# Attention and two feed-forward layers: adds out of PSUM in place of accumulating transfers, and part of a bit shift on ScalarE

## The chip, the cores and the metric

The kernel runs on one core of a Trainium2 chip. The metric is the device time of one execution in microseconds. The engines are TensorE (PE in the profile, with its weight loads as PEld), VectorE (DVE), ScalarE (ACT), GpSimd (POOL) and SyncE (SP). SP and POOL issue nearly all of the DMA transfers.

## The reference

```
# q, k, v: (4, 12, 448, 64) float32; w_in (768, 2048), w_out (2048, 768), all four weights float64
scores = 1/sqrt(64) * q @ k.T - log(448)
x = sigmoid(scores) @ v                      # heads side by side: (1792, 768)
h = x @ w_in;   x = (h - tanh(h)) @ w_out    # layer 0
h = x @ w_in2;  out = (s * relu(h)**2 + b) @ w_out2   # layer 1, float32 out
```

The weights come in as 64-bit numbers, and the kernel has to make float32 of them on the chip.

## The kernel before

**Two passes.** The four batches are taken two at a time. A pass first does the attention of two batches (12 pairs of heads, 24 heads), and then runs both feed-forward layers on their 896 tokens. Each layer goes through 16 slices of 128 hidden columns in four groups of four (`FG`). A group multiplies x by its four slices of w_in, applies the activation to get g, and multiplies g by its rows of w_out. What a group gives is added to an output y (layer 0, twelve pieces of 128x448) or z (layer 1, fourteen pieces of 128x384). In the first pass y and z lie in SBUF (both in the tile pool `yz`, so the trace calls both y in the first pass); in the second pass they are collected in device memory, in `acc`, for all but the last group.

**Products.** Every float32 product is made of three matmuls, for which each operand is split in two float32r parts: a rounded copy (`copy`, a CAST in the trace) and the difference (a subtraction on VectorE). The products with w_in, and in the second pass those with w_out too, are done by a scheme of seven products for eight blocks, which needs sums of blocks of the weights. VectorE forms these sums in place, in the buffer `wf` that holds a chunk as float32 (`w_sums`).

**Weights.** A chunk is 128 x 768 weights; a group needs eight, four of w_in and four of w_out. In the first pass `load` brings a chunk as 64-bit words into one of three `raw` buffers through SP. `conv` makes float32 of it: `y` is the view of the high words and `a` that of the low words. The high words are scaled by 2^-112 as if they were float32, which sets the exponent right; this goes to ScalarE or VectorE. The low words are shifted right by 29 bits, on VectorE. Two more VectorE instructions put the three pieces together in `wf`. Then `keep` stores the chunk in device memory, from where the second pass loads it (`f_key`). The in-place sums have to wait until that store has read `wf`. For layer 0's first chunks the sums are stored too (`wout_s`, `win_s`).

**Adding up.** `evict` in `out1` and `out2` takes a finished PSUM bank. In group 0 it is copied to y by ScalarE or VectorE. In the last group, and in the second pass, VectorE adds it to y in one instruction. In groups 1 and 2 of the first pass `add_on` is used: ScalarE or VectorE copies the bank to a buffer `t`, and GpSimd issues a transfer from SBUF to SBUF that adds t to y (24 transfers of 224 KB in layer 0 and 28 of 192 KB in layer 1).

**What sets the order.** The class `Plan` collects all operations with the keys they read and write and a cost in microseconds for each engine that can do them. For a transfer the cost is a pair: how long the queue is busy issuing it, and when it is done. `emit` then plays these costs through and writes down, engine by engine, the order in which the operations are issued; for an operation with two possible engines (`EITHER`) it picks one. TensorE's order is fixed; the costs decide what the others do when. All engines run their instructions strictly in that order. In the trace every instruction has line 85, that of the helper that records them, so rows are told apart by their tiles: `hs` is a PSUM bank of the layers, `two` and `one` those of the attention.

Of the kernel before, what the change touches and what calls it, by code (L numbers as in the profile page):

```python
# [9 lines left out]
F32 = mybir.dt.float32  # L10
F32R = mybir.dt.float32r
U32 = mybir.dt.uint32
AF = mybir.ActivationFunctionType
ALU = mybir.AluOpType
# [5 lines left out]
def tile_kernel(ctx, tc, q, k, v, w_in1, w_out1, w_in2, w_out2, s_in, b_in, out):  # L20
# [17 lines left out]
    B, H, S, D = q.shape  # L38
# [9 lines left out]
    FC = DF // P  # L48
    HM = DM // 2
# [5 lines left out]
    FG = 4  # L55
# [180 lines left out]
    def copy(e, o, t):  # L236
        (act.copy if e == "ACT" else dve.tensor_copy)(o, t)
# [287 lines left out]

    def half(nm, j, src, keys, sbuf=True):
        t, key, _ = xo[nm, j]
        do(EITHER, (0.46, 0.35 if sbuf else 0.54), lambda e: copy(e, t()[:, 0], src()), r=keys, w=[(*key, 0)])
        do("DVE", 0.54, lambda: dve.tensor_tensor(out=t()[:, 1], in0=src(), in1=t()[:, 0].bitcast(F32), op=ALU.subtract), r=[*keys, (*key, 0)], w=[(*key, 1)])

    def less(o, a, b, r, w):
# [41 lines left out]
    class Layers:  # L573
# [11 lines left out]
        def do(self, eng, cost, fn, r=(), w=()):  # L585
            do(eng, cost, fn, r, w)
# [14 lines left out]
        def conv(self, n):  # L601

            self.load(n)
            if n in self.f_of:
                return
            key = chunks[n]
            rk, k = self.raw_of.pop(n), self.f.take()
            self.f_of[n] = k
            r, t = raw_w[rk], f_t[k]
            y, a = r[:, :, 1], r[:, :, 0]  # L610

            def scale(e):
                if e == "ACT":
                    act.activation(y.bitcast(F32), y.bitcast(F32), AF.Copy, scale=2.0 ** -112)
                else:
                    dve.tensor_scalar(y.bitcast(F32), y.bitcast(F32), 2.0 ** -112, None, op0=ALU.mult)

            self.do(EITHER, (0.74, 0.47), scale, w=[("r", rk)])
            self.do("DVE", 0.47, lambda: dve.tensor_scalar(a, a, 29, None, op0=ALU.logical_shift_right), w=[("r", rk)])
            self.do("DVE", 0.88, lambda: dve.scalar_tensor_tensor(out=a, in0=y, scalar=3, in1=a, op0=ALU.logical_shift_left, op1=ALU.bitwise_or), w=[("r", rk)])  # L620
            self.do("DVE", 0.88, lambda: dve.scalar_tensor_tensor(out=t.bitcast(U32), in0=y, scalar=0x80000000, in1=a, op0=ALU.bitwise_and, op1=ALU.bitwise_or), r=[("r", rk)], w=[("f", k)])
            self.r.give(rk)

            self.keep(k, key)

        def keep(self, k, key):

            def fn():
                scratch[key] = dram.tile([P, WE], F32, name="w" + "_".join(map(str, key)))
                sp.dma_start(out=scratch[key], in_=f_t[k])  # L630

            self.do("SP", (1.9, 3.0), fn, r=[("f", k)], w=[("d", key)])

        def kept_sums(self, key):
            return key[1] == 0 and key[2] < (FG if key[0] == "in" else 2)
# [6 lines left out]
            return self.f_of.pop(n)  # L642

        def hi_lo(self, src, hi, lo, r, w, half=False):
            self.do(EITHER, (0.42, 0.3) if half else (0.74, 0.47), lambda e: copy(e, hi(), src), r=r, w=[w[0]])
            self.do("DVE", 0.47 if half else 0.88, lambda: dve.tensor_tensor(out=lo(), in0=src, in1=hi().bitcast(F32), op=ALU.subtract), r=[*r, w[0]], w=[w[1]])

        def w_whole(self, k):

# [475 lines left out]
            prod("3", "a", 1)  # L1125
            to("a", 0, 1, True)

        def add_on(self, bank, m, to, keys):

            k = self.t.take()  # L1130
            self.do(EITHER, (0.43, 0.54) if m == S else (0.38, 0.47), lambda e: copy(e, self.tt[k][:, :m], self.banks[bank][:, :m]), r=[("b", bank)], w=[("t", k)])
            self.do("POOL", (1.0, 7.0), lambda: pool.dma_start(out=to(), in_=self.tt[k][:, :m], accum_op=ALU.add), r=[("t", k)], w=keys)
            self.t.give(k)

        def out1(self, layer, grp, n, close):

            final = grp == FC // FG - 1
# [20 lines left out]
            def evict(hd, d):  # L1158
                dm = hd * 3 + d
                t = lambda i: ys_t["y"][dm][:, i]  # L1160
                yk = [cells(dm * T2 + i * S, S) for i in range(2)]
                for i in range(2):
                    bank = ps[hd, d, i]
                    if grp == 0:
                        self.do(EITHER, (0.43, 0.54), lambda e, bank=bank, i=i: copy(e, t(i), self.banks[bank]), r=[("b", bank)], w=yk[i])
                    elif not self.sb and 0 < grp < FC // FG - 1:
                        self.add_on(bank, S, lambda i=i: t(i), yk[i])
                    else:
                        self.do("DVE", 0.54, lambda bank=bank, i=i: dve.tensor_tensor(out=t(i), in0=self.banks[bank], in1=t(i), op=ALU.add), r=[("b", bank)], w=yk[i])
                    self.b.give(bank)  # L1170
                if d == 2:
                    for k in range(2):
                        self.w_done(*self.units.pop(n + 2 * hd + k))
                if not final:
                    return
                j = dm // 2
                p = self.tt
                if dm % 2 == 0:
                    k = self.y_t1 = self.t.take()
                    half("11", j, lambda: t(0), yk[0])  # L1180
                    less(lambda: p[k], lambda: t(1), lambda: t(0), [*yk[0], *yk[1]], [("t", k)])
                    half("t1", j, lambda: p[k], [("t", k)])
                    return
                k1, k2, k3, k4 = self.y_t1, *(self.t.take() for _ in range(3))
                b11, bk = (lambda: ys_t["y"][dm - 1][:, 0]), cells((dm - 1) * T2, S)
                half("21", j, lambda: t(0), yk[0])
                less(lambda: p[k2], lambda: t(1), lambda: p[k1], [*yk[1], ("t", k1)], [("t", k2)])
                half("t2", j, lambda: p[k2], [("t", k2)])
                less(lambda: p[k3], lambda: p[k2], b11, [("t", k2), *bk], [("t", k3)])
                half("t3", j, lambda: p[k3], [("t", k3)])  # L1190
                half("22", j, lambda: t(1), yk[1])
                less(lambda: p[k4], lambda: t(0), lambda: p[k2], [("t", k2), *yk[0]], [("t", k4)])
                half("t4", j, lambda: p[k4], [("t", k4)])
                for k in (k1, k2, k3, k4):
                    self.t.give(k)
# [16 lines left out]
        def out2(self, layer, grp, n, close):  # L1212
# [24 lines left out]
            def evict(hd, t):  # L1237
# [2 lines left out]
                ks = cells(t * DM + hd * HM, HM)  # L1240
                if grp == 0:
                    self.do(EITHER, (0.38, 0.47), lambda e: copy(e, zt(), self.banks[bank][:, :HM]), r=[("b", bank)], w=ks)
                elif not self.sb and 0 < grp < FC // FG - 1:
                    self.add_on(bank, HM, zt, ks)
                else:
                    self.do("DVE", 0.47, lambda: dve.tensor_tensor(out=zt(), in0=self.banks[bank][:, :HM], in1=zt(), op=ALU.add), r=[("b", bank)], w=ks)
                self.b.give(bank)
# [136 lines left out]
```

## Time and profile before

| | us |
|---|---|
| median of 3 runs | 1054.42 (1052.88 to 1054.45) |
| the profiled execution | 1049.27 |
| its span, first to last instruction | 1047.5 |
| TensorE busy | 1028.0 (98%) |
| VectorE busy | 892.0 (85%) |
| ScalarE busy | 601.1 (57%) |
| GpSimd busy | 187.9 (18%) |

The span is 1.8 us shorter than the execution. The attention of the first pass ends near 85 us, the layers of the first pass run from there to about 540 us, the attention of the second pass to about 620 us, and its layers to the end. A busy TensorE is not TensorE at its best, since matmuls are pipelined; where it waits shows in its idle time. Times in the windows view are sums over instructions of one engine within a stretch.

### The profile page before, as it was taken

The page shows a single profiled execution, that of the slowest core. Times are in us where ns is not written, and L with a number is a line of the kernel's source. Part 1 is how long each engine was busy: PE and PEld are TensorE (multiplying, and loading weights), DVE is VectorE, ACT ScalarE, POOL GpSimd, SP SyncE. Part 2 cuts the span into 40 slices and gives each one's busy share as a digit, 9 for nine tenths or more (in the row PEclk, how much of TensorE's full clock was granted, in tenths as well). Part 3 has the DMA queues.
Part 4 walks back from the last instruction along what each step waited for, and adds up shares of the span by engine and source line. Part 5 has one row for each costly group of instructions (what it writes and reads, how often), then busy time and mean ns, then how long its engine had stood idle before and what let it go on. Part 6 is the DMA issues. An engine that isn't in the chain of part 4 may idle for free.

```text
span 1047.5 us, 15848 instructions
## 1 busy us (share of the span) xinstructions
PE 1028.0 (98%) x5688; PEld 896.7 (86%) x5688; DVE 892.0 (85%) x1480; ACT 601.1 (57%) x990; POOL 187.9 (18%) x238
## 2 busy tenths in 40 slices
PE   8999999999999999899999899999999999999998
PEld 4557999898988999898985459999999999999998
DVE  4899989897999998898856689798887999898962
ACT  5776666464555665454426566656555466666650
POOL 4220001203000003122222100306060003061600
PEclk9999999999999999999999999999999999999999
DMA  6773567969722659879576503929497019293963
GB/s 154 201 189 121 166 198 208 281 193 276 213 71 98 187 178 231 235 196 284 137 227 152 179 16 123 233 92 213 104 224 215 31 38 225 80 211 84 214 170 106
DMA packets 137966, 176.92 MB, mean 169 GB/s; under 512 B 53760, under 2 KB 108800, under 8 KB 137888
## 3 DMA queue, kind: packets, MB, share of 16 engines
q1 hardware_dynamic: 111200, 135.82, 41.6%
q0 software_dynamic: 25888, 39.89, 22.0%
q8 instruction: 45, 0.74, 0.3%
q10 hardware_dynamic: 800, 0.20, 0.1%
q14 instruction: 33, 0.27, 0.1%
HBM read 103.02 MB, written 61.83 MB: 157 GB/s over the span
## 4 chain that ended last, share of the span: by engine, by line
PE 76%; DVE 14%; DMA 5%; issue 2%; ACT 1%; SPq 0%; DVEq 0%; ACTq 0%
PE hs L85 64%; PE two L85 6%; PE one L85 6%; DVE t L85 4%; DVE wf L85 3%; DVE w L85 2%; DVE raw L85 2%; DVE xo L85 1%; DVE g L85 1%; DMA win<-wf 1%; DMA raw<-in_moe_w_out_dram 1%; DVE y L85 1%; DMA raw<-in_moe_w_in_dram 1%; DMA wf<-wout 1%; ACT t L85 1%
## 5 line engine op out<-in xcount | busy, mean ns | idle before, releaser
L85 PE MATMUL hs<-xo,w 128*128 128x448 f32 x2016 | 423.7, 368 | 6.6 <-DVE t L85 5.7
L85 PEld LDWEIGHTS hs<-xo,w 128*128 128x128 f32 x2016 | 378.2, 188 | 45.5 <-DVE t L85 7.6
L85 PE MATMUL hs<-w,g 128*128 128x384 f32 x1290 | 228.1, 335 | 0.7 <-DVE w L85 0.6
L85 PE MATMUL hs<-g,w 128*128 128x448 f32 x1098 | 226.4, 366 | 0.0
L85 PEld LDWEIGHTS hs<-w,g 128*128 128x128 f32 x1290 | 224.1, 188 | 2.2 <-DVE w L85 0.9
L85 PEld LDWEIGHTS hs<-g,w 128*128 128x128 f32 x1098 | 206.1, 188 | 17.2 <-DVE g L85 0.3
L85 DVE TENSOR_TENSOR w<-wf,w 128x768 fp32r<-128x768 f32 (+1 forms) x216 | 187.7, 883 | 23.5 <-PE hs L85 11.9
L85 ACT COPY t<-hs 128x448 f32<-128x448 f32 (+2 forms) x239 | 120.1, 515 | 111.1 <-PE hs L85 99.8
L85 ACT CAST w<-wf 128x768 fp32r<-128x768 f32 (+1 forms) x177 | 137.2, 781 | 77.5 <-DVE wf L85 58.5
L85 POOL DMA_DIRECT2D acc<-t x106 | 93.6, 1227 | 318.0 <-ACT t L85 157.1
L85 POOL DMA_DIRECT2D y<-t x52 | 46.1, 985 | 371.0 <-ACT t L85 177.4
L85 DVE TENSOR_TENSOR g<-t,g 128x448 fp32r<-128x448 f32 (+2 forms) x170 | 98.6, 596 | 6.7 <-ACT g L85 6.1
L85 DVE TENSOR_TENSOR wf<-wf 128x384 f32<-128x384 f32 x168 | 93.3, 556 | 12.6 <-DMA win<-wf 7.4
L85 ACT CAST g<-t 128x448 fp32r<-128x448 f32 (+2 forms) x147 | 79.9, 552 | 33.4 <-DVE t L85 31.7
L85 ACT ACTIVATE af<-two,nlogs 128x896 f32<-128x896 f32 (+1 forms) x96 | 85.2, 919 | 8.5 <-PE two L85 6.2
L85 DVE TENSOR_TENSOR t<-hs,t 128x448 f32<-128x448 f32 x114 | 70.2, 619 | 6.2 <-PE hs L85 4.1
L85 ACT ACTIVATE raw<-raw 128x768 f32<-128x768 f32 x60 | 55.6, 926 | 33.3 <-DMA raw<-in_moe_w_out_dram 23.4
L85 DVE SCALAR_TENSOR_TENSOR raw<-raw 128x768 uint32<-128x768 uint32 x64 | 61.2, 957 | 5.5 <-ACT raw L85 3.7
L85 ACT ACTIVATE t<-t,b_sb,s_sb 128x448 f32<-128x448 f32 x64 | 48.0, 761 | 25.4 <-DVE t L85 25.1
L85 DVE TENSOR_TENSOR t<-t 128x448 f32<-128x448 f32 (+1 forms) x98 | 58.8, 603 | 4.1 <-ACT t L85 3.8
L85 DVE SCALAR_TENSOR_TENSOR wf<-raw 128x768 uint32<-128x768 uint32 x64 | 60.7, 953 | 0.7
L85 PE MATMUL two<-qt,kt 64*128 64x448 f32 x396 | 51.4, 384 | 0.1
(79 smaller groups left out, 710.8 us busy)
## 6 DMA issues: line engine op xcount, KB each, us to landing
raw<-in_moe_w_in_dram SPq DMA_DIRECT2D x32, 768.0 KB, 5.7
raw<-in_moe_w_out_dram SPq DMA_DIRECT2D x32, 768.0 KB, 7.9
wf<-wout SPq DMA_DIRECT2D x36, 384.0 KB, 6.6
win<-wf SPq DMA_DIRECT2D x32, 384.0 KB, 3.5
wout<-wf SPq DMA_DIRECT2D x32, 384.0 KB, 6.3
wf<-win SPq DMA_DIRECT2D x32, 384.0 KB, 4.3
acc<-t POOLq DMA_DIRECT2D x51, 224.0 KB, 7.7
acc<-t POOLq DMA_DIRECT2D x55, 192.0 KB, 8.0
```

Source lines behind the costliest of these rows:

```text
L85: return lambda *a, **kw: tc.keep_in_program_order(getattr(self.engine, name)(*a, **kw))
```

## The change

Three things change. In groups 1 and 2 of the first pass a finished bank is added to y by VectorE, as in the last group, and `add_on` is gone. The shift of the low words may be done by ScalarE too: it reads the word as a number, multiplies by 2^-29 x (1 - 2^-16), takes away 0.5 - 2^-14 and rounds to a whole number on writing, which leaves the top three bits. And seven costs that the planner uses are other numbers.

```diff
     def half(nm, j, src, keys, sbuf=True):
-        do(EITHER, (0.46, 0.35 if sbuf else 0.54), ...)
+        do(EITHER, (0.46, 0.38 if sbuf else 0.6), ...)
...
         def conv(self, n):
...
-            self.do(EITHER, (0.74, 0.47), scale, w=[("r", rk)])
-            self.do("DVE", 0.47, lambda: dve.tensor_scalar(a, a, 29, None, op0=ALU.logical_shift_right), w=[("r", rk)])
+            self.do(EITHER, (0.83, 0.47), scale, w=[("r", rk)])
+
+            def top(e):
+                if e == "ACT":
+                    act.activation(a, a, AF.Copy, bias=-0.5 + 2.0 ** -14, scale=2.0 ** -29 * (1 - 2.0 ** -16))
+                else:
+                    dve.tensor_scalar(a, a, 29, None, op0=ALU.logical_shift_right)
+
+            self.do(EITHER, (0.83, 0.47), top, w=[("r", rk)])
...
         def keep(self, k, key):
...
-            self.do("SP", (1.9, 3.0), fn, r=[("f", k)], w=[("d", key)])
+            self.do("SP", (1.9, 5.2), fn, r=[("f", k)], w=[("d", key)])
...
         def hi_lo(self, src, hi, lo, r, w, half=False):
-            self.do(EITHER, (0.42, 0.3) if half else (0.74, 0.47), ...)
-            self.do("DVE", 0.47 if half else 0.88, ...)
+            self.do(EITHER, (0.42, 0.5) if half else (0.74, 0.47), ...)
+            self.do("DVE", 0.52 if half else 0.88, ...)
...
-        def add_on(self, bank, m, to, keys):
-
-            k = self.t.take()
-            self.do(EITHER, (0.43, 0.54) if m == S else (0.38, 0.47), lambda e: copy(e, self.tt[k][:, :m], self.banks[bank][:, :m]), r=[("b", bank)], w=[("t", k)])
-            self.do("POOL", (1.0, 7.0), lambda: pool.dma_start(out=to(), in_=self.tt[k][:, :m], accum_op=ALU.add), r=[("t", k)], w=keys)
-            self.t.give(k)
-
...
             def evict(hd, d):
...
-                    elif not self.sb and 0 < grp < FC // FG - 1:
-                        self.add_on(bank, S, lambda i=i: t(i), yk[i])
                     else:
                         self.do("DVE", 0.54, lambda bank=bank, i=i: dve.tensor_tensor(out=t(i), in0=self.banks[bank], in1=t(i), op=ALU.add), r=[("b", bank)], w=yk[i])
...
             def evict(hd, t):
...
-                elif not self.sb and 0 < grp < FC // FG - 1:
-                    self.add_on(bank, HM, zt, ks)
                 else:
                     self.do("DVE", 0.47, lambda: dve.tensor_tensor(out=zt(), in0=self.banks[bank][:, :HM], in1=zt(), op=ALU.add), r=[("b", bank)], w=ks)
```

With new costs and other operations the planner writes another order on VectorE, ScalarE, SP and POOL; TensorE's stays. Three places matter below. The first is on VectorE, late in group 1 of layer 1 of the first pass (422 to 431 us of the trace). The names are buffers: raw is a chunk of 64-bit words, wf a chunk as float32, w its split parts, hs a PSUM bank, y the output; the rows with 128x3x128 are the in-place sums. Before:

```order
L85 SCALAR_TENSOR_TENSOR wf_83<-raw_106 128x768
L85 COPY t_100<-hs_949 128x384
L85 SCALAR_TENSOR_TENSOR wf_84<-raw_104 128x768
L85 TENSOR_TENSOR w_78<-wf_83,w_992 128x768
L85 TENSOR_TENSOR w_79<-wf_84,w_79 128x384
L85 TENSOR_SCALAR raw_105<-raw_105 128x768 x2
L85 SCALAR_TENSOR_TENSOR raw_105<-raw_105 128x768
L85 TENSOR_TENSOR wf_84<-wf_84 128x3x128
L85 TENSOR_TENSOR wf_84<-wf_83,wf_84 128x3x128
L85 SCALAR_TENSOR_TENSOR wf_81<-raw_105 128x768
L85 TENSOR_TENSOR wf_83<-wf_84,wf_83 128x3x128
L85 TENSOR_TENSOR wf_83<-wf_83 128x3x128
```

Here one bank is copied by VectorE, the TENSOR_SCALAR row is two shifts, and the four sums in wf_84 and wf_83 stand among conversions. The same place in the changed kernel:

```order
L85 TENSOR_TENSOR y_140<-hs_962,y_140 128x384
L85 SCALAR_TENSOR_TENSOR raw_104<-raw_104 128x768
L85 SCALAR_TENSOR_TENSOR wf_84<-raw_104 128x768
L85 SCALAR_TENSOR_TENSOR wf_83<-raw_106 128x768
L85 TENSOR_TENSOR y_140<-hs_956,y_140 128x384
L85 TENSOR_TENSOR y_140<-hs_957,y_140 128x384
L85 TENSOR_TENSOR w_78<-wf_83,w_1001 128x768
L85 TENSOR_TENSOR w_79<-wf_84,w_79 128x384
L85 TENSOR_TENSOR y_140<-hs_960,y_140 128x384
L85 SCALAR_TENSOR_TENSOR raw_105<-raw_105 128x768
L85 SCALAR_TENSOR_TENSOR wf_81<-raw_105 128x768
L85 TENSOR_TENSOR wf_84<-wf_84 128x3x128
```

The shifts are gone from here, and four adds of a bank into y stand between the conversions, ahead of the weight parts and sums that follow them.

The second place is on SP, at the boundary of the passes. rawqkv is a set of q, k and v for the second pass's attention, wout_..._s are stored sums of w_out, and wf<-win_0_1 is a load of weights for layer 0 of the second pass. Before, behind the last q and k loads:

```order
L85 DMA rawqkv_4619<-in_k_dram 64x2x64
L85 DMA out_0_dram<-y_140 128x384
L85 DMA wout_0_0_1_s_4953<-wf_82 128x768
L85 DMA wout_0_1_0_s_4968<-wf_83 128x768
L85 DMA wout_0_1_1_s_4981<-wf_84 128x768
L85 DMA wf_82<-win_0_1_0_583 128x768
L85 DMA wf_83<-win_0_0_0_s_831 128x768
L85 DMA wf_84<-win_0_1_0_s_856 128x768
```

The three stores of sums stand behind the loads of q and k and right ahead of the weight loads that need their buffers. In the changed kernel the stores stand far ahead, among the last output stores of the first pass, in front of all those loads of q and k:

```order
L85 DMA wf_81<-win_0_0_0_697 128x768
L85 DMA wout_0_0_1_s_4434<-wf_82 128x768
L85 DMA out_0_dram<-y_140 128x384
L85 DMA wout_0_1_0_s_4456<-wf_83 128x768
L85 DMA out_0_dram<-y_140 128x384 x3
L85 DMA wout_0_1_1_s_4486<-wf_84 128x768
L85 DMA rawqkv_4208<-in_q_dram 128x3x64 x2
L85 DMA rawqkv_4208<-in_q_dram 64x2x64
L85 DMA rawqkv_4208<-in_k_dram 128x3x64 x2
L85 DMA rawqkv_4208<-in_k_dram 64x2x64
```

At the place where they were there are now only the weight loads:

```order
L85 DMA out_0_dram<-y_140 128x384
L85 DMA wf_82<-win_0_1_0_560 128x768
L85 DMA wf_83<-win_0_0_0_s_857 128x768
L85 DMA wf_84<-win_0_1_0_s_923 128x768
L85 DMA out_0_dram<-y_140 128x384
```

The load wf_82<-win_0_1 now follows an output store, and the stores whose buffers it and the next two loads use are all earlier.

The third place is on VectorE, where that load is used (579 to 588 us of the trace). two is a PSUM tile with q and k of the next pair of heads, which go to qt and kt in two parts each; one is the PSUM tile of a pair's result, whose bank is free once xo and y are written from it. Before:

```order
L85 CAST qt_4611<-two_4623 128x448
L85 CAST kt_4613<-two_4623 128x448
L85 COPY t_103<-two_4623 128x512
L85 TENSOR_TENSOR qt_4611<-two_4623,qt_4611 128x448
L85 TENSOR_TENSOR kt_4613<-two_4623,kt_4613 128x448
L85 CAST w_78<-wf_82 128x384
L85 TENSOR_TENSOR w_78<-wf_82,w_78 128x384
L85 TENSOR_TENSOR one_4626<-one_4626,t_102 128x224
L85 CAST xo_87<-one_4626 128x448
L85 TENSOR_TENSOR xo_87<-one_4626,xo_87 128x448
```

The half-width cast of wf_82 stands behind qt and kt of the next pair, with two instructions between it and xo. In the changed kernel:

```order
L85 CAST w_78<-wf_82 128x384
L85 CAST qt_4560<-two_4572 128x448
L85 CAST kt_4562<-two_4572 128x448
L85 COPY t_103<-two_4572 128x512
L85 TENSOR_TENSOR qt_4560<-two_4572,qt_4560 128x448
L85 TENSOR_TENSOR kt_4562<-two_4572,kt_4562 128x448
L85 TENSOR_TENSOR w_78<-wf_82,w_78 128x384
L85 TENSOR_TENSOR w_80<-wf_83,w_79 128x768
L85 TENSOR_TENSOR one_4575<-one_4575,t_102 128x224
L85 CAST xo_87<-one_4575 128x448
L85 TENSOR_TENSOR xo_87<-one_4575,xo_87 128x448
```

It now stands ahead of qt and kt, and a full-width difference of wf_83 has come between it and the work on one.

## Rows read from the trace of the kernel before

**Rows 1.** Part 1 of the page: busy us (share of the span) xinstructions.

```profile
PE 1028.0 (98%) x5688; PEld 896.7 (86%) x5688; DVE 892.0 (85%) x1480; ACT 601.1 (57%) x990; POOL 187.9 (18%) x238
```

**Rows 2.** TensorE's timeline: start, length, instructions [idle before <-what ended it].

```profile
205.89 15.14 PE L85 MATMUL hs<-xo,w 128*128 128x448 f32 x72 [0.62 <-ACT t L85]
...
314.24 19.71 PE L85 MATMUL hs<-xo,w 128*128 128x448 f32 x93 [0.98 <-DVE t L85]
...
334.69 1.51 PE L85 MATMUL hs<-w,g 128*128 128x384 f32 x5 [0.57 <-DVE w L85]
...
433.57 16.42 PE L85 MATMUL hs<-xo,w 128*128 128x448 f32 x72 [2.83 <-DVE t L85]
...
487.37 3.88 PE L85 MATMUL hs<-xo,w 128*128 128x448 f32 x18 [0.80 <-DVE t L85]
...
505.03 2.09 PE L85 MATMUL hs<-xo,w 128*128 128x448 f32 x9 [0.37 <-DVE t L85]
...
589.13 4.46 PE L85 MATMUL one<-af,rawqkv 128*64 128x448 f32 x20 [2.94 <-DVE y L85]
```

**Rows 3.** Windows: us, engines' busy us (xinstructions), PEclk, DMA share, GB/s.

```profile
434.00:436.00 2.00, 2.00 (x10) 1.83 (x9) 2.00 (x4) 1.58 (x2) 0.00 (x0) 0.77 1.02 404
436.00:438.00 2.00, 2.00 (x7) 1.80 (x6) 1.86 (x4) 0.53 (x1) 0.00 (x0) 0.50 1.06 408
```

**Rows 4.** The same view, longer stretches of the first pass.

```profile
180.00:215.00 35.00, 34.38 (x169) 31.40 (x168) 29.94 (x47) 18.99 (x30) 9.56 (x11) 1.00 1.03 271
400.00:438.00 38.00, 35.17 (x186) 33.76 (x185) 30.21 (x44) 16.80 (x28) 12.48 (x14) 0.96 1.07 285
465.00:495.00 30.00, 28.83 (x157) 27.33 (x156) 25.54 (x40) 12.72 (x19) 10.38 (x12) 1.00 1.09 285
270.00:340.00 70.00, 68.29 (x331) 61.43 (x331) 69.62 (x119) 39.35 (x66) 0.00 (x0) 1.00 0.35 110
```

**Rows 5.** DMA, 180 to 215 us (packets, MB, share; median us to landing), then 275:345.

```profile
q0 software_dynamic: 1728, 2.75, 45.2%
...
raw<-in_moe_w_out_dram SPq DMA_DIRECT2D x4, 768.0 KB, 11.4
...
win<-wf SPq DMA_DIRECT2D x4, 384.0 KB, 6.4
...
raw<-in_moe_w_out_dram SPq DMA_DIRECT2D x4, 768.0 KB, 5.3
...
win<-wf SPq DMA_DIRECT2D x4, 384.0 KB, 3.6
```

**Rows 6.** Chain of waits ahead of two stalls: start, us, what.

```profile
424.38 4.96 DMA win<-wf
...
483.27 12.13 DMA raw<-in_moe_w_out_dram
```

**Rows 7.** Groups by shape: xcount | busy us, mean ns | idle before.

```profile
L85 DVE TENSOR_TENSOR y<-hs,y 128x448 f32<-128x448 f32 x26 | 15.5, 619 | 0.5 <-PE hs L85 0.4
...
L85 DVE TENSOR_TENSOR y<-hs,y 128x384 f32<-128x384 f32 x14 | 7.7, 555 | 10.1 <-PE hs L85 10.1
...
L85 DVE TENSOR_SCALAR raw<-raw 128x768 uint32<-128x768 uint32 x64 | 35.7, 558 | 6.8 <-DMA raw<-in_moe_w_out_dram 4.3 <-DMA raw<-in_moe_w_in_dram 2.5
...
L85 ACT ACTIVATE raw<-raw 128x768 f32<-128x768 f32 x60 | 55.6, 926 | 33.3 <-DMA raw<-in_moe_w_out_dram 23.4 <-DMA raw<-in_moe_w_in_dram 9.5
...
L85 ACT CAST w<-wf 128x768 fp32r<-128x768 f32 x147 | 122.4, 836 | 66.7 <-DVE wf L85 53.7 <-PE hs L85 10.4 <-DMA acc<-t 1.1
...
L85 ACT ACTIVATE t<-t,b_sb,s_sb 128x448 f32<-128x448 f32 x64 | 48.0, 761 | 25.4 <-DVE t L85 25.1
```

**Rows 8.** The pass boundary: VectorE's and SyncE's timeline.

```profile
585.77 0.55 DVE L85 CAST w<-wf 128x384 fp32r<-128x384 f32 x1 [3.93 <-DMA wf<-win]
...
577.22 1.70 SPq L85 DMA_DIRECT2D wout_s<-wf  x3
581.44 0.32 SPq L85 DMA_DIRECT2D wf<-win  x1
```

More of the change, by code (lines that the diff above doesn't have):

```diff
@@ L527, in half @@
         t, key, _ = xo[nm, j]
-        do(EITHER, (0.46, 0.35 if sbuf else 0.54), lambda e: copy(e, t()[:, 0], src()), r=keys, w=[(*key, 0)])
+        do(EITHER, (0.46, 0.38 if sbuf else 0.6), lambda e: copy(e, t()[:, 0], src()), r=keys, w=[(*key, 0)])
         do("DVE", 0.54, lambda: dve.tensor_tensor(out=t()[:, 1], in0=src(), in1=t()[:, 0].bitcast(F32), op=ALU.subtract), r=[*keys, (*key, 0)], w=[(*key, 1)])
@@ L644, in hi_lo @@
         def hi_lo(self, src, hi, lo, r, w, half=False):
-            self.do(EITHER, (0.42, 0.3) if half else (0.74, 0.47), lambda e: copy(e, hi(), src), r=r, w=[w[0]])
-            self.do("DVE", 0.47 if half else 0.88, lambda: dve.tensor_tensor(out=lo(), in0=src, in1=hi().bitcast(F32), op=ALU.subtract), r=[*r, w[0]], w=[w[1]])
+            self.do(EITHER, (0.42, 0.5) if half else (0.74, 0.47), lambda e: copy(e, hi(), src), r=r, w=[w[0]])
+            self.do("DVE", 0.52 if half else 0.88, lambda: dve.tensor_tensor(out=lo(), in0=src, in1=hi().bitcast(F32), op=ALU.subtract), r=[*r, w[0]], w=[w[1]])
         def w_whole(self, k):
```

## The prediction

> **What bounds the kernel now.** I read part 1 of the page first. TensorE is busy 1028.0 of 1047.5 us, so only the 19.5 us in which it stands still, and what a lowered clock adds, can be won; VectorE at 85% and ScalarE at 57% have room on average [rows 1]. So the next view was TensorE's timeline, for the matmuls that had to wait [rows 2]. The reader should see that the stalls are few, that they lie in the first pass (85 to 540 us) and at its end, and that nearly all were ended by a VectorE or ScalarE result. In the first pass they are 0.62 us at 205.9, 0.98 at 314.2, 0.57 at 334.7, 2.83 at 433.6, and three from 0.80 to 0.37 us between 487 and 505 (0.80, 0.37, 0.37). At the pass boundary 2.94 us end at 589.1. After the 2.83 us stall the granted clock was 0.77 for 2 us and 0.50 (the 1.2 GHz level) for the next 2 us, though matmuls ran all the time [rows 3]: 2 x 0.23 + 2 x 0.50 = 1.46 us more.
>
> What comes before these stalls? The stretches that end in the first, the 2.83 and the 0.80 us stall (and a fourth like them between 235 and 270) have the DMA engines full (1.03 to 1.09 of 16 engines) and VectorE not full: 30.21 of 38 us in the one that ends worst [rows 4]. In them run the accumulating transfers. In 180 to 215 the software queue, that is those transfers, takes 45.2% of the DMA engines' time, and a load of 64-bit w_out words lands after 11.4 us, a store of a converted chunk after 6.4 us. In 275 to 345, where no accumulating transfer runs, the same load takes 5.3 us and the same store 3.6 us [rows 5]. The chain of waits runs through such transfers right ahead of two of the stalls: 4.96 us of a win store before 433.6, 12.13 us of a w_out load before the last ones [rows 6]. So these stalls are late weights: VectorE can't form the sums in a wf buffer before its store has read it, nor start a chunk before its load lands. The stretch 270 to 340 is the other kind: DMA at 0.35, VectorE at 69.62 of 70 us, and 0.98 + 0.57 us lost.
>
> **The change part by part.**
> *The 52 accumulating transfers go.* Each was a copy out of PSUM by ScalarE or VectorE and a transfer; now VectorE adds the bank to y itself: 28 x 555 ns + 24 x 619 ns = 30.4 us more [rows 7]. In the instruction order 39 copies leave ScalarE and 13 leave VectorE (9 of 384 columns, 4 of 448), which at the same durations is 7.5 us less for VectorE. GpSimd's issuing goes too; nobody on the path waits for it.
> *The shift of the low words.* All 64 were VectorE's, at 558 ns; in the new order 17 instructions of that form are left on VectorE instead of 68 (4 of the 68 were scalings), and ScalarE has 111 on raw instead of 60. So VectorE loses 51 x 0.558 = 28.5 us, and its sum for the kernel is 30.4 - 7.5 - 28.5 = -5.6 us. ScalarE gains 51 times a form that the trace doesn't show (whole numbers in and out). Its nearest row is the scaling of the same words at 926 ns; a cast of the same size at 836 ns is the lower bound, and the activation with scale and bias at 761 ns for 448 columns, or 1.30 us for 768, the upper. I take 0.926: 47.2 us (42.6 to 66.6). Even with none of the 39 copies taken off, ScalarE then stands at 648 us, 62%, and at the upper bound at 668 us, 64%: it does not become the bound. The two ScalarE passes of a chunk now follow each other where VectorE's shift ran beside the scaling, so a chunk is ready up to 0.93 us later. I cost that at nothing: it is hidden by the three raw buffers that load ahead, and in the four stretches by a load that lands 6.1 us sooner. Without that cover it would be 0.93 us at each of the four other groups' ends, 3.7 us.
> *VectorE group by group.* The two groups of each layer that had the transfers get 12 x 0.619 = 7.4 us (layer 0) or 14 x 0.555 = 7.8 us (layer 1), less 3.6 us of shifts (51 / 8 x 0.558) and 1.2 or 2.5 us of copies. The stretches go from 29.94 to about 32.6 of 35 us, from 30.21 to 31.9 of 38 and from 25.54 to 27.3 of 30 [rows 4]. They still fit. The final group of layer 0 gets only the relief of 3.6 us.
> *The planner's costs* (a store of a chunk 5.2 instead of 3.0, a scaling 0.83 instead of 0.74, a half-width cast 0.50 instead of 0.30) are nearer to the durations [rows 5, 7]. They move the sums in wf behind more other work, among it the new adds, as the rows of the order in the section on the change show.
>
> *The sum.* Term A, the stalls behind slow transfers: 0.62 + 2.83 + 0.80 + 0.37 + 0.37 = 4.99 us and 1.46 us of clock, 6.45 us. I take all of it, since what makes these transfers slow loses nearly half of its DMA time; what is late next there is VectorE.
> *Term B*, the full stretch of layer 0: 1.55 us against a relief of 3.6 us; I take half, 0.8, because an order written anew does not put its relief where the stall was.
> *Term C*, what is new: a bank is now freed by VectorE alone, in its order, ahead of weight work behind it. The trace shows that form twice without transfers: layer 0's final group lost 1.55 us at a full VectorE, and the same timeline has no stall in layer 1's final group, from 505.0 on. So 0 to 1.55 us for each of four groups, 0 to 6.2; with VectorE at 84 to 93% I take 0.25 each, 1.0.
> *Term D*, the pass boundary: the three sum stores that held up the load of the next weights (issued at 577.22) stand in the new order ahead of the second pass's loads of q and k, and no longer behind them, so the load, issued at 581.44 [rows 8], can go right behind the last output store, about 4.2 us sooner. But the half-width cast that waits for it (3.93 us idle on VectorE) now stands ahead of the next pair's five instructions on PSUM and not behind them, and a full-width difference has come in, all of it before the result that TensorE waited for. Gain and loss about cancel: 0, with -2.94 - 1.46 = -4.4 us and, if TensorE waits for those casts too, some +1 as its ends.
>
> -6.45 - 0.8 + 1.0 + 0 = -6.25 us. On the profiled execution's 1049.27 us (span 1047.5 and 1.8 around it) that is 1043.0. The median of the runs, 1054.42, lies 5.15 above that execution, and I move the difference over: **1048.2 us**. With C at its least and B whole it is 1046.4 (-8.0), with C at its most and B at nothing 1054.2.
>
> **The rivals.**
> *The transfers were not the limit.* In the four stretches the DMA engines moved 271 to 285 GB/s, but in 436 to 438 us the core moved 408 GB/s [rows 3, 4]. If bytes are the measure, there was room, the late weights come from the order of loads and stores, and A stays: -0.8 + 1.0, so 1054.6 us, no change. Against it stand the same load at 11.4 and 5.3 us. For it: landings depend on when a load is issued, and the order is new. The Trainium skill, "Perfetto Trace Analysis", section "Identifying the Most-Contended Engine", speaks for this rival: it wants the DMA side judged by memory bandwidth used, and not by occupancy, as sixteen engines make occupancy mislead. By that rule 66 to 70% of the rate reached elsewhere is no bound and the forecast would be 1054.6; the trace agrees that the rate was below its best, and not that the transfers were quick.
> *VectorE becomes the bound where the adds are* (the slower side). Its place is the four group ends, where PSUM adds, each waiting for TensorE, stand in VectorE's order among the chunk conversions. If one of them waits, the weights behind it come late, as at 433.6. Price: 2.83 us at each of the four ends, 11.3 us, in place of A: -6.45 - 0.8 + 11.3 = +4.1, so 1058.5 us (1064.3 with 1.46 us of clock at each). It decides from the point where VectorE's work fills the stretch, as it did in 270 to 340; I work out 84 to 93%, so it takes 7% more work or waiting than that. For it: 465 to 495 comes out at 27.3 of 30.
> *The boundary stall goes as well.* The stores are out of the way and the load lands early enough: 1046.4 - 4.4 = 1042.0 us.
> *The shift does not move, or ScalarE is late with the casts behind it*: the order shows that 51 move; ScalarE at 62% leaves no price beyond the 3.7 us above.
>
> **How the numbers follow.** A measurement of this kernel tells 0.2%, 2.1 us, from no change. The forecast has 0.57 (1045.5 to 1051.5), the boundary case 0.12 (down to 1042.0), transfers not the limit 0.19 (1052.3 to 1056.5), VectorE as bound 0.12 (above that). All of the first two is faster than 1052.3, and I count a little of the third below it: faster 0.70, same 0.18, slower 0.12. For 8 in 10 I take 1042.5 to 1055.5.
>
> **What would show it.** Right: in the stretches around 180 to 215 and 400 to 438 the DMA share well below 1, w_out loads landing near 5.5 us, no matmul waiting 2.83 us near 433 and the clock at 1.00 there; VectorE near 92% busy in them; ScalarE's rows on raw 111 near 926 ns; the stall near 314 smaller or gone. Wrong: TensorE stalls of over 1 us that end on a VectorE add into y or on a w behind one (the slower rival), or loads that land sooner with the stalls still there (the first rival). A boundary stall gone would show D mis-sized.

## The result and the profile after

The changed kernel takes 1033.81 us (median of 4 runs, 1033.22 to 1035.47) against 1053.65 us of the kernel before beside it (4 runs, 1051.61 to 1054.45): a ratio of 0.9823, 95% interval 0.980 to 0.9845. It is faster by 19.8 us. The prediction had the direction and its main mechanism, but its 1048.2 us held only about a third of the gain, and its range reached down only to 1042.5.

The profiled execution took 1033.57 us (span 1031.8, mean granted clock 1.0). Part 1 of its page, to set against [rows 1]: TensorE stands still for 8.2 us of the span in place of 19.5.

```profile
PE 1023.6 (99%) x5688; PEld 896.3 (87%) x5688; DVE 884.8 (86%) x1469; ACT 617.1 (60%) x1001; POOL 141.8 (14%) x186
```

The windows (us, then busy us of PE, PEld, DVE, ACT and POOL with their counts, granted clock, DMA share, GB/s), which answer to [rows 3, 4]:

```profile
180.00:215.00 35.00, 35.00 (x175) 32.43 (x174) 32.35 (x49) 19.74 (x29) 0.00 (x0) 1.00 0.64 201
...
400.00:438.00 38.00, 38.00 (x202) 36.20 (x202) 36.03 (x58) 22.36 (x32) 0.00 (x0) 1.00 0.57 182
...
465.00:495.00 30.00, 30.00 (x155) 28.03 (x154) 27.14 (x42) 19.03 (x29) 3.03 (x5) 1.00 0.50 156
...
270.00:340.00 70.00, 69.85 (x348) 64.18 (x347) 69.29 (x118) 41.94 (x67) 0.00 (x0) 1.00 0.29 90
...
434.00:436.00 2.00, 2.00 (x12) 1.81 (x11) 2.00 (x4) 2.00 (x4) 0.00 (x0) 1.00 0.25 46
```

TensorE fills every one of the stretches to within 0.15 us, at the full clock; the DMA share is 0.50 to 0.64 where it was 1.03 to 1.09; VectorE is at 32.35 of 35 us (the prediction said 32.6) and 27.14 of 30 (27.3). In 400 to 438 it is at 36.03 where 31.9 was forecast, because TensorE got through 202 matmuls there in place of 186, and VectorE's work came with them. The stretch of the kernel before that holds the same 202 matmuls has 34.57 us of VectorE, so the change added 1.5 us where 1.7 was forecast:

```profile
404.94:447.39 42.45, 39.62 (x202) 37.49 (x202) 34.57 (x54) 21.62 (x36) 10.12 (x12) 0.96 0.90 234
```

The DMA view of 180 to 215 us shows loads and stores as quick as those of a stretch without accumulating transfers [rows 5]:

```profile
raw<-in_moe_w_out_dram SPq DMA_DIRECT2D x3, 768.0 KB, 5.1
...
win<-wf SPq DMA_DIRECT2D x2, 384.0 KB, 2.6
```

TensorE's timeline has no stall of over 0.15 us between 85 and 540 us. Around the pass boundary it shows these (start, length, count, [idle before <-what ended it]), which answer to the last row of [rows 2]:

```profile
571.62 1.49 PE L85 MATMUL two<-qt,kt 64*128 64x448 f32 x12 [0.18 <-DVE kt L85]
...
575.12 3.01 PE L85 MATMUL one<-af,rawqkv 128*64 128x448 f32 x20 [0.30 <-DVE y L85]
...
600.32 3.01 PE L85 MATMUL one<-af,rawqkv 128*64 128x448 f32 x20 [0.41 <-DVE xo L85]
```

The groups by shape, for [rows 7] (count, busy us, mean ns): the shift on ScalarE, whole numbers in and out, costs the same as the scaling, 913 against 916 ns; I had taken 926.

```profile
L85 ACT ACTIVATE raw<-raw 128x768 f32<-128x768 f32 x58 | 53.1, 916 | 13.5 <-DMA raw<-in_moe_w_in_dram 7.4 <-DMA raw<-in_moe_w_out_dram 5.8
...
L85 ACT ACTIVATE raw<-raw 128x768 uint32<-128x768 uint32 x53 | 48.4, 913 | 0.0
...
L85 DVE TENSOR_TENSOR y<-hs,y 128x448 f32<-128x448 f32 x50 | 29.9, 617 | 3.6 <-PE hs L85 3.4
```

### The profile page after: what moved, and what is told of

The parts are those of the page before. It is cut to its first block, busy times and chain, and to the rows that moved or that the text cites. A ratio compares the mean times of both kernels' runs of the same rounds, so it can differ in the third digit from the quotient of the medians.

```text
span 1031.8 us, 15681 instructions
## 1 busy us (share of the span) xinstructions
PE 1023.6 (99%) x5688; PEld 896.3 (87%) x5688; DVE 884.8 (86%) x1469; ACT 617.1 (60%) x1001; POOL 141.8 (14%) x186
## 4 chain that ended last, share of the span: by engine, by line
PE 87%; DVE 9%; issue 1%; ACT 1%; DMA 0%; SPq 0%; DVEq 0%; ACTq 0%
PE hs L85 75%; PE two L85 6%; PE one L85 5%; DVE t L85 3%; DVE w L85 1%; DVE wf L85 1%; DVE xo L85 1%; DVE y L85 1%; DVE g L85 1%; DVE raw L85 1%; DMA wf<-win 0%; ACT t L85 0%; DVE qt L85 0%; DVE kt L85 0%; ACT af L85 0%
## 5 line engine op out<-in xcount | busy, mean ns | idle before, releaser
L85 ACT CAST w<-wf 128x768 fp32r<-128x768 f32 (+1 forms) x173 | 133.9, 780 | 91.1 <-DVE wf L85 59.6
L85 ACT COPY t<-hs 128x448 f32<-128x448 f32 (+1 forms) x200 | 100.6, 516 | 94.9 <-PE hs L85 88.2
L85 ACT ACTIVATE raw<-raw 128x768 f32<-128x768 f32 (+1 forms) x111 | 99.2, 915 | 13.5 <-DMA raw<-in_moe_w_in_dram 7.4
L85 ACT CAST g<-t 128x448 fp32r<-128x448 f32 (+1 forms) x143 | 77.7, 551 | 26.1 <-DVE t L85 24.3
L85 POOL DMA_DIRECT2D rawqkv<-in_v_dram x36 | 22.9, 642 | 482.6 <-DVE t L85 424.2
L85 DVE TENSOR_TENSOR y<-hs,y 128x448 f32<-128x448 f32 (+1 forms) x92 | 52.8, 587 | 18.6 <-PE hs L85 18.5
```

The costliest lines, as they stand in the source:

```text
L85: return lambda *a, **kw: tc.keep_in_program_order(getattr(self.engine, name)(*a, **kw))
```

## The experiments

The change has three parts: the accumulating transfers become adds on VectorE ("adds"), the shift may go to ScalarE ("shift"), and the planner gets other costs ("costs"). e1 to e4, e5 to e8 and e9 to e12 were run as three groups, each on one chip and beside runs of its own of the kernel before; so versions are compared by their ratio to it.

| kernel | parts | median us (range, runs) | ratio, 95% |
|---|---|---|---|
| e1_small | transfers of 64 columns | 1037.27 (1036.03–1037.95, 4) | 0.9890, 0.9870–0.9910 |
| e2_plain | transfers that don't add | 1035.65 (1035.18–1037.69, 4) | 0.9874, 0.9852–0.9897 |
| e3_adds | adds | 1040.10 (1037.47–1040.84, 4) | 0.9914, 0.9891–0.9937 |
| e4_costs | costs | 1050.25 (1046.16–1055.27, 10) | 1.0002, 0.9980–1.0023 |
| e5_after_again | all | 1034.06 (1032.82–1035.19, 5) | 0.9847, 0.9823–0.9871 |
| e6_no_costs | adds, shift | 1038.13 (1035.10–1040.10, 6) | 0.9884, 0.9859–0.9910 |
| e7_no_shift | adds, costs | 1038.30 (1037.31–1039.91, 6) | 0.9892, 0.9868–0.9917 |
| e8_shift_only | shift | 1044.36 (1042.87–1046.64, 8) | 0.9947, 0.9929–0.9966 |
| e9_layer0_transfers | adds in layer 1 | 1042.60 (1038.10–1045.84, 5) | 0.9929, 0.9904–0.9954 |
| e12_store_cost_old | all but one cost | 1034.03 (1032.76–1036.69, 4) | 0.9859, 0.9837–0.9881 |

The kernel before, in the three groups: 1049.97 (1046.65–1053.15), 1050.55 (1045.84–1054.87) and 1049.90 (1047.63–1051.67).

### What in the transfers costs: e1_small and e2_plain

The edits are shown shortened, here and below.

```diff
-dma_start(out=to(), in_=tt[k][:, :m], accum_op=ADD)
+dma_start(out=to()[:, :64], in_=tt[k][:, :64], accum_op=ADD)   # e1_small
+dma_start(out=to(), in_=tt[k][:, :m])                          # e2_plain
```

> The kernel before, in the same order on every engine, but each of the 52 accumulating transfers carries 64 columns in place of 448 or 384 (so y and z are not complete). Theory 1 (the DMA load of these transfers makes loads and stores of weights late): the stalls between 205 and 505 us go, 7 to 9 us with the lowered clock, the loads of w_out in 180 to 215 us land near 5.5 us in place of 11.4, and the boundary stall of 2.94 us stays; 1041 to 1046 us. Rival (the order and the planner's costs): nothing changes in the order, so 1052 to 1055 us, stalls at the same places.

> The kernel before, in the same order, but the 52 transfers overwrite y and z in place of adding to them (so the sums are not complete): the same bytes out, without the read of the destination. If the bytes that are moved are what loads the DMA engines, as before: 1051 to 1055 us. If it is the adding in the transfer, it comes near the run with small transfers, 1041 to 1046 us, with the software queue's share in 180 to 215 us well under 45%.

Both keep the instruction order of before, on every engine, and both lose the stalls: TensorE is busy for the whole of 180 to 215 and 400 to 438 us, with only 0.70 and 0.57 us left in the full stretch near 311 and 332. Both came out faster than any of the ranges expected, and the boundary stall, which was to stay in e1, went as well (0.18 us in e1, none over 0.15 in e2). The software queue in 180 to 215 us, first of e1_small, then of e2_plain (packets, MB, share of 16 engines' time; KB each, us to landing):

```profile
q0 software_dynamic: 1728, 0.39, 13.6%
...
y<-t POOLq DMA_DIRECT2D x11, 32.0 KB, 4.4
```

```profile
q0 software_dynamic: 756, 2.69, 20.0%
...
raw<-in_moe_w_out_dram SPq DMA_DIRECT2D x4, 768.0 KB, 6.8
...
y<-t POOLq DMA_DIRECT2D x10, 224.0 KB, 6.2
```

Against the 1728 packets, 2.75 MB and 45.2% of before [rows 5], e1_small moves a seventh of the bytes in as many packets and takes 13.6%; e2_plain moves the same bytes in 756 packets and takes 20.0%. So it is the adding of whole pieces, which more than doubles both the packets and the DMA engines' time for the same bytes. And e2_plain, whose window of 180 to 215 us follows, decides between DMA time and bandwidth: it moved 280 GB/s in this stretch without a stall, where before moved 271 with one. What parted the two was the DMA share, 0.84 against 1.03. By bandwidth, which the Trainium skill, "Perfetto Trace Analysis", section "Identifying the Most-Contended Engine", wants in place of occupancy for the DMA side, they would have looked alike; but the same sentence goes on to ask which DMA resource actually binds, and the prediction had left that half out.

```profile
180.00:215.00 35.00, 35.00 (x175) 32.44 (x174) 31.63 (x49) 20.51 (x32) 5.38 (x10) 1.00 0.84 280
```

### The parts alone: e3_adds and e4_costs

```diff
-elif not self.sb and 0 < grp < FC // FG - 1:
-    self.add_on(bank, ...)          # e3_adds: these lines in out1 and out2 only
-self.do("SP", (1.9, 3.0), fn, ...)
+self.do("SP", (1.9, 5.2), fn, ...)  # e4_costs: the changed costs only
```

> Only the adds by VectorE in place of the transfers; the shift stays on VectorE and the planner's costs stay as before. Theory 1: the late weights go as with small transfers, but VectorE has 23 us more work in the first pass, so layer 0's full stretch (0.98 and 0.57 us) stays or grows and some new waits on VectorE appear: 1040 to 1048 us. Rival (order and costs): 1050 to 1056 us. Rival (VectorE is the bound without the shift's relief): over 1054 us, with stalls that end on an add into y.

> Only the planner's new costs (store of a chunk 5.2, scaling 0.83, half-width cast 0.50 and the others); transfers and shift as before. Theory 1: the late weights stay as the DMA engines stay full in the four stretches, 1048 to 1054 us; the boundary stall goes if the stores of sums have moved ahead of the q and k loads here too (3 to 4 us of it). Rival (order and costs do it): 1034 to 1045 us and no stall over 1 us in 180 to 505 us though the DMA share stays near 1.

The costs alone gain nothing: e4_costs keeps the DMA share at 0.98 in 180 to 215 us, and the late stalls. Four rows of its timeline:

```profile
207.54 13.28 PE L85 MATMUL hs<-xo,w 128*128 128x448 f32 x63 [2.33 <-ACT t L85]
...
434.24 20.05 PE L85 MATMUL hs<-xo,w 128*128 128x448 f32 x90 [3.86 <-DVE t L85]
...
492.26 3.98 PE L85 MATMUL hs<-xo,w 128*128 128x448 f32 x18 [1.40 <-ACT t L85]
...
586.42 3.01 PE L85 MATMUL one<-af,rawqkv 128*64 128x448 f32 x20 [0.91 <-DVE xo L85]
```

The last row stands for the boundary: in e4's order a load wf<-win is issued ahead of the three stores of sums, and in place of the 2.94 us stall there are 0.77 us at 548.71 and these 0.91.

The adds alone bring somewhat over half of the gain, though VectorE is then as good as full, as two windows of e3_adds show:

```profile
180.00:215.00 35.00, 35.00 (x175) 32.43 (x174) 34.62 (x54) 18.06 (x28) 0.00 (x0) 1.00 0.61 198
...
400.00:438.00 38.00, 38.00 (x206) 36.52 (x205) 37.48 (x61) 17.77 (x26) 0.00 (x0) 1.00 0.66 211
```

With 34.62 of 35 and 37.48 of 38 us, TensorE still never waits in them. It loses 1.99 us (0.64, 0.19 and 1.16) between 312 and 333, in the stretch without adds that was full already. So a VectorE at 99% for 35 us did not become the bound by itself in this execution. It is the fastest of e3's four, 1037.47 us; the others took 1040.04 to 1040.84, and what they lost no trace shows.

### The parts in pairs: e5_after_again, e6_no_costs, e7_no_shift, e8_shift_only

e5_after_again is the changed kernel unaltered. The others, against the kernel before:

```diff
+self.do(EITHER, (0.83, 0.47), top, w=[("r", rk)])   # the shift: e6, e8
-    self.add_on(bank, ...)                          # the adds: e6, e7
+self.do("SP", (1.9, 5.2), fn, ...)                  # the costs: e7
```

> The changed kernel once more, unaltered, beside the three partial versions that follow and on their chip, so that each step from one to the next is a difference of paired runs. Both theories expect 0.982 of the kernel before (1031 to 1035 us), no stall of TensorE over 0.2 us between 85 and 540 us. If the gain of 20 us were an accident of one set of runs, the ratio would be 0.988 or more here.

> The adds on VectorE and the shift free to go to ScalarE, with the planner's costs left as before. Theory 1 (the transfers' load is all that mattered, the shift makes room on VectorE, the costs do nothing, as they did nothing alone): within 2 us of the changed kernel, ratio 0.981 to 0.984, and the small stall of some 0.4 us behind the copies at the start of the second pass is back, since the planner's cost for the scratch store is the old one. Theory 2 (the costs order the eviction chains once VectorE carries the adds): 1036 to 1041 us, with stalls of 0.5 to 1.2 us at 312 to 335 us behind VectorE, as in the run with the adds alone.

> The adds on VectorE with the new costs, the shift kept on VectorE. Theory 1 (the shift is worth what VectorE's full stretches lose): 1037 to 1041 us, as with the adds alone; VectorE at 34.3 to 34.8 of 35 us in 180 to 215 us and 1.0 to 1.2 us stalls at 312 to 335 us behind VectorE. Theory 2 (the costs are what removed those stalls): 1031 to 1035 us with VectorE as full as that.

> Only the shift freed for ScalarE; the accumulating transfers stay, and the costs are as before. Theory 1 (the load of the accumulating transfers makes the late weights, which a free VectorE does not bring sooner): 1048 to 1054 us, ratio 0.997 to 1.003, transfers at 1.0 us of busy time per us in 180 to 215 us and weight loads landing in 10 us or more. Theory 2 (VectorE being full was the larger part of the lateness): 1040 to 1045 us, VectorE at 26 to 28 of 35 us there and the stalls of 3 us at 434 and 589 us gone.

e5 repeats the gain, with 16.5 us against its own runs of before. That is some 3 us less than at first; the changed kernel took the same time (1034.06 and 1033.81 us), and it was the kernel before that was quicker here (1050.55 against 1053.65). e2, which only takes the adding out of the transfers, gained 14.3 us beside its own runs of before: most of the gain lies there. e7 is as its theory 1 said in time and on VectorE (34.51 of 35 us in 180 to 215); its stalls behind VectorE at 326 and 333 are only 0.31 and 0.56 us, and 0.68 and 1.29 stand at 535 and 573. e8 went against theory 1 in time: the shift alone gives 0.53%, some 5.6 us, with the transfers still there, and its 1044.36 us and VectorE's 27.39 of 35 us are as theory 2 had them. Its window of 180 to 215 us and a row of its timeline:

```profile
180.00:215.00 35.00, 32.70 (x161) 29.68 (x160) 27.39 (x40) 18.66 (x29) 10.47 (x12) 1.00 1.00 253
```

```profile
267.25 16.41 PE L85 MATMUL hs<-xo,w 128*128 128x448 f32 x72 [2.67 <-ACT t L85]
```

The DMA share is 1.00 and loads of w_out still land after 10.8 us, as theory 1 had it, and stalls of 2.03 and 2.67 us stand at 205 and 267; but the one near 433 has shrunk to 0.57 and that of the boundary is gone. So the transfers make the weights late, and how much of the lateness reaches TensorE depends on something else as well: VectorE's room, or the new order that came with it, which e8 does not tell apart. e6 has the time of its theory 2, without any of the stalls that theory 2 named; e11 below shows why, for two of its executions.

### Stage by stage: e9_layer0_transfers

```diff
 # out2 (layer 1) only; out1 keeps its transfers
-elif not self.sb and 0 < grp < FC // FG - 1:
-    self.add_on(bank, HM, zt, ks)
```

> The accumulating transfers stay in layer 0 (24 of 448 columns) and only layer 1's 28 become adds on VectorE; shift and costs as before. Theory 1 (each late weight comes from the transfers of its own stretch): 180 to 215 us still at 0.95 to 1.05 us of DMA time per us, weight loads landing in 10 us or more and a stall of 0.5 to 2.5 us near 206 us; but 400 to 438 at 0.6 to 0.7, no stall over 0.6 us between 400 and 510, clock 1.00 there, and the stall at the pass boundary gone; 1043 to 1047 us. Theory 2 (lateness is carried on: what layer 0 loses pushes layer 1 and the boundary): the stall near 433 us, or that at the boundary, still over 1.5 us; 1047 to 1051 us.

Two windows and a row of the timeline of e9_layer0_transfers:

```profile
180.00:215.00 35.00, 34.17 (x169) 31.34 (x168) 30.20 (x47) 19.10 (x31) 9.04 (x11) 1.00 1.04 279
...
400.00:438.00 38.00, 38.00 (x207) 36.59 (x206) 37.48 (x60) 17.77 (x25) 0.00 (x0) 1.00 0.65 215
```

```profile
582.95 4.61 PE L85 MATMUL one<-af,rawqkv 128*64 128x448 f32 x20 [3.05 <-DVE y L85]
```

In layer 0, where the transfers stay, the DMA share is 1.04, w_out lands after 11.4 us, and 0.83, 0.20 and 0.64 us are lost; in layer 1, without them, 0.65, 6.0 us, and no stall from 400 to 510. The stalls of the first pass are made where the transfers run. The boundary stall did not obey: 3.05 us, and theory 1 had it gone. This trace is of the slowest of e9's five executions (1045.84 us, with a median of 1042.60 and 1038.10 as the fastest), so it is not known whether the others had that stall. VectorE's timeline shows that the lateness begins before the boundary, at the end of layer 1:

```profile
527.76 2.34 DVE L85 TENSOR_TENSOR wf<-wf 128x384 f32<-128x384 f32 x4 [2.62 <-DMA wf<-wout]
...
579.59 0.55 DVE L85 CAST w<-wf 128x384 fp32r<-128x384 f32 x1 [4.04 <-DMA wf<-win]
```

The load wf<-wout that the first row waits for landed after 7.4 us. In e1, e2 and e3, which also issue the stores of sums right ahead of the load of weights, it landed after 3.2 to 4.6 us and VectorE did not wait for it.

### The kernel before once more: e10_before_again

> The kernel before once more, unaltered, for a second trace of it. Theory 1 (what its runs differ by is the stalls behind the accumulating transfers, which fall out differently each time): the stalls between 200 and 510 us stand at the same places, and their sum differs from the first trace's 5.97 us by about as much as the two times differ. Theory 2 (the runs differ by something outside the stalls): the same stalls to within 0.3 us each, whatever the time.

It took 1053.56 us, near the 1053.65 to 1054.42 that the runs beside the first two profiles had as medians, though the eight runs of before beside it took only 1047.63 to 1051.67; the execution on which the prediction was built took 1049.27. Some of its stalls, to set beside [rows 2]:

```profile
202.12 3.91 PE L85 MATMUL hs<-xo,w 128*128 128x448 f32 x18 [0.62 <-ACT t L85]
...
207.63 13.28 PE L85 MATMUL hs<-xo,w 128*128 128x448 f32 x63 [1.59 <-ACT t L85]
...
265.33 13.03 PE L85 MATMUL hs<-xo,w 128*128 128x448 f32 x63 [0.97 <-ACT t L85]
...
279.09 2.12 PE L85 MATMUL hs<-xo,w 128*128 128x448 f32 x9 [0.72 <-ACT t L85]
...
438.19 16.42 PE L85 MATMUL hs<-xo,w 128*128 128x448 f32 x72 [3.66 <-DVE t L85]
...
593.13 4.39 PE L85 MATMUL one<-af,rawqkv 128*64 128x448 f32 x20 [2.52 <-DVE y L85]
```

All of its stalls of over 0.15 us between 200 and 510 us add up to 10.62 us. In the first trace they were 6.54 (the expectation's 5.97 left out the 0.57 at 334.7). The difference is 4.08 us, and that of the two times 4.29: theory 1 in size. The places are the same only in part. From 202 to 221 us e10 lost 2.56 us where the first trace has 0.62; from 260 to 279 it lost 1.96, where the first trace has no stall at all, though the stretch before was as loaded as the others there (its window follows, DMA share 1.04); the stall near 434 is 0.83 us longer, and that near 314 is 0.72 shorter.

```profile
235.00:270.00 35.00, 34.86 (x169) 31.36 (x168) 28.06 (x41) 17.80 (x29) 10.32 (x12) 1.00 1.04 276
```

### Two paces of TensorE: e11_no_costs_again

> Again the adds and the shift with the old costs, whose six times lay in two groups (1035.1 to 1036.8 and 1039.4 to 1040.1). If TensorE's two steady paces (203 or 207 ns from one matmul of 448 columns to the next) are what parts them, a time near 1036 goes with 203 ns in most of 105 to 305 and 690 to 820 us, and one near 1040 with 207 ns, with the same stall of 0.97 us near 105 us in both. Otherwise the pace is 207 ns whatever the time.

The same kernel took 1034.76 us this time, and 1040.10 in its first profiled execution. Windows and one row of the timeline, first of e6_no_costs, then of e11_no_costs_again:

```profile
110.00:160.00 50.00, 50.00 (x243) 45.43 (x243) 42.31 (x62) 33.41 (x53) 0.00 (x0) 1.00 0.62 185
...
220.00:270.00 50.00, 50.00 (x244) 45.43 (x243) 45.80 (x69) 27.15 (x39) 0.00 (x0) 1.00 0.64 203
```

```profile
105.61 5.81 PE L85 MATMUL hs<-xo,w 128*128 128x448 f32 x27 [0.97 <-ACT t L85]
```

```profile
110.00:160.00 50.00, 50.00 (x249) 46.34 (x248) 43.08 (x63) 34.26 (x54) 0.00 (x0) 1.00 0.62 190
...
220.00:270.00 50.00, 50.00 (x248) 46.34 (x247) 46.81 (x70) 28.57 (x42) 0.00 (x0) 1.00 0.65 206
```

```profile
105.77 5.71 PE L85 MATMUL hs<-xo,w 128*128 128x448 f32 x27 [0.98 <-ACT t L85]
```

Both fill TensorE in both windows at the full clock, yet one issues 243 or 244 matmuls in 50 us and the other 249 or 248. From start to start it is a steady 207 ns in e6 from 105 to 310 and from 690 to 820 us, and in e11 it averages 203 ns (203, 202, 203, 199, 207, over and over). Read matmul by matmul, that is worth 3.9 us in the first stretch and 2.3 in the second; e11 gives back 0.61 in a stall near 312. The stall of 0.97 us stands in both, so it does not by itself decide the pace that follows.

### One cost set back: e12_store_cost_old

```diff
-self.do("SP", (1.9, 5.2), fn, r=[("f", k)], w=[("d", key)])
+self.do("SP", (1.9, 3.0), fn, r=[("f", k)], w=[("d", key)])
```

> The changed kernel with one of its costs set back, that of the scratch store (3.0 in place of 5.2). If the costs' worth of some 4 us hangs on the store's: 1036 to 1040 us, and the stall of about 0.97 us near 105 us, which both kernels with the shift and old costs show, is back. If it hangs on the other costs: 1032 to 1035 us and no stall near 105 us.

1034.03 us and no stall near 105: what the costs are worth does not hang on the store's. The stall of 0.96 to 0.98 us near 105 us is in e6, e8 and e11, which have the shift with the old costs, and in no other kernel here; the remaining costs (scaling, half-width casts) take it away. The rest of the 4 us between the medians of e5 and e6 can't be told from the pace: their intervals overlap, and e11's 1034.76 lies among e5's times.

## Why the prediction was wrong in size

Of the 14.4 us between the forecast of 1048.2 and the 1033.81 measured, 5.15 are the difference between the profiled execution and the median, which the prediction carried over, and some 9 are in its terms and in what it left out.

TensorE's order is the same in both kernels, so the lead of the changed one can be read matmul by matmul from the two timelines. It grows to 15.7 us at the end of the span; all but 0.4 us of that come in these steps (each read to about 0.1 us):

| place in before | lead gained | predicted |
|---|---|---|
| A: 205.9; 433.6; the lowered clock behind it; 487 to 505 | 0.79 + 3.0 + 1.4 + 1.97 = 7.16 | 6.45 |
| B: 314, 335 | 1.0 + 1.07 = 2.07 | 0.8 |
| C: new waits at the adds | none | −1.0 |
| D: 589, with clock | 2.40 + 1.45 = 3.85 | 0 |
| 207 for 203 ns from 206 to 276 us | 1.5 | – |
| small stalls near 257 and 543 | 0.38 + 0.32 = 0.70 | – |

Two rows of the kernel before belong to this table: the third stall of 487 to 505 us, which term A counts, and the window behind the boundary stall, with the clock that D lost there:

```profile
491.62 13.03 PE L85 MATMUL hs<-xo,w 128*128 128x448 f32 x63 [0.37 <-DVE t L85]
```

```profile
589.00:591.00 2.00, 1.87 (x6) 0.77 (x8) 2.00 (x5) 0.00 (x0) 0.00 (x0) 0.50 0.91 326
```

*The transfers were the limit: right.* e1, e2 and e9 show it, and the first rival (bytes as the measure) falls with e2. Term A on the profiled execution was sized well.

*"The median of the runs, 1054.42, lies 5.15 above that execution, and I move the difference over": the step that failed most.* It took the difference for something that the change leaves alone. The medians show that it is not: before took 1053.65, 1050.55 and 1049.90 us in three sets of runs, and the changed kernel beside it 1033.81, 1034.06 and, with one cost set back, 1034.03. For one execution e10 shows what such a difference is made of: stalls of the first pass, 4.08 of 4.29 us, and 1.96 of them in the fourth loaded stretch, which term A put at nothing because the one trace has no stall there. None of the runs behind the median of 1054.42 was traced; that they were like e10, and term A at the median some 4 us larger than at the execution that I read, is inferred. The spread points the same way, more weakly: 6.5, 9.0 and 4.0 us over 13, 13 and 8 runs of before, 9.1 over 10 of e4 and 7.7 over 5 of e9, against 1.9 to 3.9 for the kernels without the adding of whole pieces (4 to 6 runs each), but for e6's 5.0 with its two paces; e8, with the transfers, has only 3.8 over 8. The profiled execution of after lies 0.24 us below its median.

*Term D, "gain and loss about cancel: 0": wrong, 3.85 us came, near its lower end of −4.4.* SyncE's and VectorE's timelines of after, for [rows 8]:

```profile
564.05 0.43 SPq L85 DMA_DIRECT2D wf<-win  x1
```

```profile
568.30 0.55 DVE L85 CAST w<-wf 128x384 fp32r<-128x384 f32 x1 [0.80 <-DMA wf<-win]
```

The load is issued 17.4 us earlier. TensorE's lead (11.6 us at 543) explains the larger part, and the other 5.8 are more than the 4.2 that were forecast; VectorE waits 0.80 us for the load in place of 3.93. The price that I set against it, the cast standing ahead of five instructions on PSUM, came to at most 0.48 us (0.18 and 0.30 at 571.62 and 575.12). From the matmul of 542.94 to that of 589.13 TensorE takes 46.18 us in before, 45.76 in e10 and 46.30 in e9, but 43.18 in e8 (transfers kept, order new) and 43.43, 43.19 and 43.71 in e1, e2 and e3 (the stores where before has them, the load of the transfers gone). So either the new order or the lighter load removes the stall. What made e9's loads late at the end of its layer 1, which has no transfers, stays open.

*Term C, +1.0: not there.* No matmul waits over 0.2 us behind an add; even e3's profiled execution, with VectorE at 99%, had none in the four groups. The slower rival falls with it.

*Term B, half of 1.55: the whole of it went*, and the shift's relief of VectorE is what took it: between 311 and 340 us the kernels without the shift lose 0.83 to 1.99 us (e1 to e4, e7, e9, e10), those with it 0 to 0.61 (e5, e6, e8, e11, e12). I had halved it on a general doubt.

*Not in the prediction:* the pace. The sum of C, D, B, A and what was left out is 9.0 us, and 1043.0, the forecast for the profiled execution, less 9.0 is 1034.0; it took 1033.57.

## What to carry to other kernels

Before a forecast is moved from a profiled execution to the median, ask what the runs differ by: if the spread comes from the stalls that the change removes, it goes with them, and the slow executions gain most. A stretch as loaded as those that stall is not safe because one trace has no stall in it. An accumulating transfer took more than twice the DMA engine time of a plain one of the same bytes here, and others pay it as late weights; adds on a nearly full VectorE cost TensorE less here than those. Where a term lies between 0 and a known stall, and the order visibly moves the load that ends it, 0 is one end of it and not its middle.

## What was not expected of the hardware

The adding in a transfer raised its packets from 756 to 1728 and its share of DMA time from 20.0% to 45.2% for 2.69 and 2.75 MB. TensorE at full clock and without a wait ran 448-column matmuls at either of two steady paces, 203 or 207 ns, for 70 to 200 us on end, in the same kernel; between two executions of one kernel it made 6.2 us of 1035, more than most terms above. What sets the pace stays open. ScalarE's shift of whole numbers through its conversion took 913 ns, as much as a scaling of floats (916).
